# A new hand-over-hand order for the same operations of a recurrence-and-gated-MLP kernel

## The chip, the cores and the metric

The kernel runs on one core of a Trainium2 chip. The metric is the device time of one execution in microseconds (us). Below, TensorE is also PE, VectorE is DVE, ScalarE is ACT, GpSimd is POOL, and SyncE (SP) is the engine whose queue issues nearly all DMAs.

## The reference

Four batches, eight heads, 768 steps, head size 48. First a gated linear recurrence, then an MLP with a spatial mix:

```python
for t in range(S):
    state = alpha[:, :, t, :, None] * state + einsum('bhd,bhe->bhde', k[:, :, t], v[:, :, t])
    y[:, :, t] = einsum('bhd,bhde->bhe', q[:, :, t], state)
x = y.transpose(0, 2, 1, 3).reshape(B, S, H * D)      # 4 x 768 x 384
h = maximum(x @ w_in, 0)                              # 384 -> 1024
u, v = h[..., :512], h[..., 512:]
v_n = (v - mean(v)) / sqrt(var(v) + 1e-6)             # over the features
v_s = einsum('ts,bsd->btd', w_spatial, v_n) + b_spatial[None, :, None]
out = (u * v_s) @ w_out                               # 512 -> 384
```

## The kernel before

**Chunks and pairs.** The recurrence is done in chunks of 128 steps, six to a batch, 24 in all (number `i`). The first eight chunks are loaded and worked on two at a time as pairs 0 to 3 (`pair`, one 384 KB load for each of alpha, k, q, v), the other 16 singly (`first`, 192 KB loads). For a chunk the kernel loads alpha, k, q and v (`ac`, `kc`, `qc`, `vc`), takes the logarithm of alpha (`ln`), sums it along the steps with a matmul (`cum`), takes the exponent with both signs (`einv`, `eexp`), scales k and q (`kt`, `qt`), casts v (`vb`), transposes k and q on TensorE (`tr`, `trk`) and copies the transposes out of PSUM (`ev`), multiplies them (`sc`), masks the product (`m`), and makes `y` from the masked product (`ya` for a pair), v and the state before the chunk. The state goes on by `upd` (matmul), `z` (add), `S` (decay) and `sb` (cast). A `y` is cast (`xs`), transposed (`xt`) and copied (`xe`) as the MLP's input. Names of pair operations carry the pair and the half: `qtp/0/1`.

**The MLP.** For each batch: `v` (relu of the second half, token by feature), its statistics `bn`, `rs` and normalisation `vn`, `u` (relu of the first half, feature by token), `s` (the spatial matmul, with the bias added on the way out of PSUM), `g` (product with u), and `o` (the last matmul) with its store `st`. The very last output tile is split in two halves `oh`. Weights come in six 768 KB pieces: `w_in` in two halves, `w_sp` in three, `w_out`; each piece is cast to bf16 in slices (`cast`), and the spatial weights are transposed (`wt`, copied out by `we`).

**What sets the order.** Nothing is left to a scheduler. The kernel builds a list of 1141 operations, each with the engines that may do it, what it depends on, and a function that emits its instructions. Then `replay` walks through the string `PLAN`. A word such as `D65` means: emit operation 65 on the engine of the letter, P TensorE, D VectorE, A ScalarE, G GpSimd, S SyncE's issue of a DMA, Q its landing (emits nothing). So the order of the words of one letter is the order of that engine's instructions; how words of different letters are mixed changes nothing but the turn of shared buffers. Every engine works through its own list in order and waits where an operand is late.

**Buffers that tie the engines.** PSUM is eight banks taken in turn (`bank`), in the order of TensorE's list: a matmul whose bank still waits for its reader waits too. Loads go into three rotating buffers for each of alpha, k, q and v (a buffer holds two chunks), so a load can be issued only when the buffer's last reader is through. SyncE issues loads and stores in one list.

**Idle matmuls.** A word of TensorE may carry numbers, as in `P43:512:512:192`. Before that operation's matmuls, `bank` emits one fp32 matmul of `junk` by `junk` for each number, with so many columns; its result is overwritten. In the profile these matmuls are line L188.

```python
        for cols in fill:
            n = cols // 4
            nc.tensor.matmul(
                out=flat[:, 0:cols].rearrange("p (a b) -> p a b", a=4), lhsT=junk,
                rhs=junk[:, None, 0:n].to_broadcast([128, 4, n]), start=True, stop=True)
```

**Lines that are met below.** L435 issues the pair loads, L446 is `lnp`, L455 `cump`, L463 `einvp`, L484 `qtp`, L477 `ktp`, L547 `updq`, L577 `sc` of a pair, L588 its mask, L604 `ya`, L822 all matmuls of the MLP, L834 `wt`, L887 `bn`, L919 `vn`, L968 the exit of `s`, L981 `g`, L198 copies on ScalarE, L200 copies on VectorE and GpSimd.

Of the kernel before, what the change touches and what calls it, by code (L numbers as in the profile page):

```python
# [9 lines left out]
FP32 = mybir.dt.float32  # L10
# [44 lines left out]
LETTERS = {"P": "PE", "D": "DVE", "A": "ACT", "G": "POOL", "S": "SP", "Q": "DMA"}  # L55

PLAN = """
G32 S34 Q33 S36 G0 S38 S40 Q35 D1 Q37 S94 A42 D2 Q39 S96 P43:512:512:192 P53:64 A44 A45 G46 Q41 S98 A54 A55 D47 G56
D57 P51:512 Q95 P49 S100 P59:64 P61 A58 G48 D60 A50 D52 P63:192 Q97 S163 A62 P247 D65 A102 P71 D248 P74 D72 A64 Q99
S167 P103:96 G66 P113 D73 A104 A114 D68 D76 A115 Q101 P249 S165 G116 A105 A250 D117 G106 D107 P121:512 Q164 S169 D75  # L60
A122 P111:64 G67 P109 D112 P119 A110 G69 D120 Q168 S4 P131:192 D70 P134 G108 P77 G118 D133 G3 P123:128 A171 Q166
D132 S307 D125 A124 A78 P172 D136 P81 G126 P182 A173 Q170 S9 D135 P79 A183 D127 A82 P137 A174 Q5 D128 A184 S311 P142
D176 P138 G185 P83 A139 D175 A80 P140 A84 D186 P178 A143 P180 D179 A177 G187 P188 P190 Q308 S309 D189 G129 P144 P192
D181 A145 D191 A141 G6 D194 A193 A8 P197 D7 Q10 P200 G195 D199 P85 S14 A315 G196 D198 P157 A86 G130 D201 P316 A158
P146 D202 Q312 A317 D159 A318 P203 A147 P204 P208 D87 P88 A205 Q310 A209 G11 P206 D12 P326 A89 D13 P210 A207 D320
P151 S18 Q15 A211 D148 S313 P212 A327 S367 G319 A328 P324 D152 P223 A213 D330 G329 P215 A160 D90 A325 Q19 P334 S371
P322 A216 P221 D162 G16 A224 D217 P153 A222 P332 G17 A91 D323 P229 A335 P225 D92 Q314 S22 D231 A154 P149 D93 A333
G20 D214 P232 A226 P227 A150 Q368 D230 S369 P155 D234 A228 D161 A233 P235 D21 Q372 A218 S409 D237 P238 A236 D219
P344 G321 A156 Q23 D239 P255 S446 D220 G331 P259 D345 A375 P376 D346 P336 A377 A378 A380 P260 D338 Q370 S373 A240
D381 P256 A337 D261 A24 P263 G339 Q410 D257 S411 P264 D25 G379 P241 Q447 D341 P347 A242 S448 D265 P251 A243 G342  # L70
D349 Q374 P244 P383 G340 S413 A245 D246 P252 D348 A417 G262 P275 Q412 A385 S415 D253 P276 D384 G258 A382 Q449 P350
D277 A454 S450 P390 A351 G343 P267 D391 Q414 P418 S480 G278 D392 P354 P352 A419 P279 Q416 A353 S26 G421 P268 A355
P386 A420 A422 P356 D269 Q451 G266 P393 S482 A357 D387 P280 A394 D423 G388 P455 Q481 D281 S484 P395 A457 P425 A456
G389 P361 D427 A424 Q27 D397 G458 A396 S452 P358 D426 A459 A362 D460 P398 G254 A359 D363 P428 A399 P462 G270 P432
D429 A488 P271 D433 A463 G430 Q483 S577 P401 D464 P489 D434 A28 G31 P407 Q485 A490 G30 S486 D400 P272 A492 P435 A402
G491 Q453 D29 P405 S581 A436 D273 P283 G282 A408 D493 Q578 S579 P437 P469 A284 G274 D438 P495 A406 D470 P403 Q487
A496 S611 G461 D471 P287 A439 G431 A497 Q582 D404 P291 S583 A288 D360 P465 P498 Q580 A585 S648 P472 D466 A292 D500
P586 G494 A364 P440 Q612 G467 D499 A587 S690 P295 A473 G468 D366 A588 A590 Q584 S615 P474 A441 G589 P501 D475 D591
P299 Q649 A502 D442 S728 A476 P503 A296 P593 G592 P477 A619 Q691 D505 D504 S613 A300 D594 P517 D365 A478 Q616 P596
D595 S650 P506 A443 D597 A479 D518 P513 Q729 D445 S652 A507 P600 D444 P620 A508 D602 Q614 P519 S692 A621 P533 D509  # L80
A656 P303 Q651 S694 A514 D601 P515 A510 Q653 A622 P525 A698 D512 S617 D511 A624 P529 G623 D516 A520 Q693 P657 S654
P534 A304 D625 G598 A659 A658 P526 D535 Q695 G599 A661 S732 P699 D527 P530 A701 A700 G660 P545 Q618 A703 D531 S730
A736 P627 G536 P603 D629 Q655 P546 S762 A604 D704 G528 P537 A628 D662 Q733 P538 S696 D547 G626 P605 P664 D539 G702
A606 P634 Q731 A607 P630 S766 A665 P541 D631 G663 A666 D635 P737 Q763 G632 P542 S858 A738 D636 G548 A739 P671 A741
P706 Q697 D543 S892 P667 A708 G532 P608 D742 A707 D672 Q767 P521 S764 G740 A609 P637 D633 A770 P549 Q859 A638 S734
D668 P522 D673 P550 Q893 G705 D523 S862 P639 P744 D551 A640 P713 G524 A641 Q765 D746 P674 A745 S860 D714 P771 G669
A675 P642 D715 A772 Q735 G670 S768 A774 P751 P676 A643 P553 G540 D678 Q863 D677 A866 S864 D775 P709 P716 A554 G773
D752 P679 Q861 A717 S929 D753 A900 G544 P557 A680 D710 Q769 D610 S896 P777 G711 A558 P718 P867 A743 G712 Q865 P561
D719 A869 D779 S933 A868 D720 A681 P747 G552 D778 P686 Q930 D644 S894 P721 A871 G870 A562 P754 D748 Q897 A722 D872
S971 P565 G749 A755 D687 G750 A645 Q934 P780 P874 S931 A566 D782 P756 P569 G776 A757 A723 Q895 D781 G873 S975 P573  # L90
D876 A758 A875 P783 D724 Q972 S898 P682 A784 A570 P881 D646 Q932 P785 P759 S973 D787 A786 D883 A574 P788 A937 Q976
D882 S935 A760 P796 D683 A789 P684 Q899 D761 S1012 A797 P877 P800 A685 D790 Q974 A725 P901 S1008 P688 A903 A801 D647
P794 A979 Q936 D726 S1042 P938 A791 D727 P798 D878 A902 Q1013 D792 P810 A940 A905 S1046 D793 G904 P802 A939 D795
P980 Q1009 D906 G879 S1010 P803 A981 P811 G941 A799 D804 Q1043 A942 P806 S977 D689 A982 G805 A984 P807 D812 Q1047
P884 S571 D943 P822 G907 A885 D985 P823 G813 Q1011 D808 S1044 P908 P886 G983 P945 A910 D887 Q978 P814 D909 S1014
A888 D824 P911 A946 G809 P815 D912 Q572 A947 P889 S1048 D816 G944 A1016 Q1045 S575 D880 P987 A890 G817 P915 P952
A988 D916 Q1015 P1017 G913 P830 A1050 D989 A1019 G914 P834 A1018 D917 Q1049 A1021 P1051 D953 G825 P838 A1052 Q576
D954 A835 P948 G1020 P831 A1054 D949 P918 D832 G950 P818 A919 D1022 G986 P819 A839 D1055 G951 P920 P1024 D820 A921
P994 A1025 G1053 D922 P990 P826 D996 A1026 P955 G1023 D995 P827 G833 A956 D991 P1031 D828 P957 P1057 G992 A959 D1032
P923 A958 G821 A1059 D1033 P960 A924 G829 P997 A1058 D925 P967 A998 G993 P1027 A961 P999 P1060 D1028 A968 P842 D962  # L100
G1029 A1000 A1001 P963 G1030 A843 D1061 P1002 A1056 S844 D1062 A964 P1034 S305 A1003 D891 P850 S836 Q845 A1035 S840
P1063 D1004 Q306 P846 A1064 Q837 A926 P1065 P1036 A847 P965 D1067 Q841 D1037 A1038 D1066 P854 D928 D966 P1068 A851
D927 A1005 P969 A1069 D1006 P1074 D1007 P1039 D1070 P1078 A1040 P1080 A855 D1041 P1076 A970 S856 P1090 S297 D1075
A1071 P1094 S285 D1079 A1077 Q857 P1082 S289 D1072 P1106 Q298 D1073 S301 D1081 P1086 Q286 S567 P1087 Q290 S563 P1083
D1088 Q302 S852 P1095 G1089 Q568 P1091 S559 D1096 P1102 Q564 S293 D1092 G1097 P1098 D1084 Q853 S848 P1103 D1093 Q560
G1085 S555 P1099 D1104 Q294 P1107 D1105 P1113 Q849 D1100 Q556 P1117 A1114 D1108 G1101 P1110 D1109 S1115 A1118 P1111
S1119 P1121 D1112 Q1116 P1137 A1122 Q1120 P1125 D1138 S1123 P1133 S1139 A1126 P1129 D1134 Q1124 S1127 S1135 A1130
Q1140 S1131 Q1128 Q1136 Q1132
"""


# [13 lines left out]
def kernel(  # L125
# [14 lines left out]
    B, H, S, D = q.shape  # L140
# [20 lines left out]
    io_pool = ctx.enter_context(tc.tile_pool(name="io", bufs=IO))  # L161
# [146 lines left out]
    T = {}  # L308
# [319 lines left out]
    def first(i):  # L628
# [3 lines left out]
        st = T[i]  # L632
        P = float(10 * i)

        def load(name, src):
            def emit(_):
                if i % 2 == 0:
                    T[i + 1][name + "2"] = st[name + "2"] = io_pool.tile([128, 2, H, D], FP32, name=name)
                t = st[name] = st[name + "2"][:, i % 2]
                nc.sync.dma_start(out=t, in_=src[b, :, t0:t0 + C, :].rearrange("h s d -> s h d"))  # L640
            return emit
# [453 lines left out]
    for b in range(B):  # L1095
        for c in range(NCH):
            i = b * NCH + c
# [50 lines left out]
```

## Time and profile before

| what | value |
|---|---|
| median of 3 runs | 145.32 us (145.25 to 145.40) |
| span of the profiled execution, first to last instruction | 142.9 us |
| granted TensorE clock | 1.000 |
| busy: TensorE matmuls | 132.9 us, 93% |
| busy: VectorE | 122.2 us, 85% |
| busy: ScalarE | 108.2 us, 76% |
| busy: GpSimd | 86.0 us, 60% |
| DMA moved | 28.6 MB, mean 200 GB/s |

The profile does not give a separate time for the profiled execution. Its span is 142.9 us, and the runs lie 2.4 us above that; this is what start and end of a program add around the first and last instruction. The spans of matmuls overlap each other, as they are pipelined, so a busy share of TensorE in the nineties means that a next matmul nearly always follows at once.

### The profile page before, as it was taken

How to read it: one execution, taken by the hardware profiler on the slowest of the kernel's cores; microseconds unless marked ns; L12 is line 12 of the kernel's file. 1: busy time of each engine (PE TensorE's matmuls, PEld its weight loads, DVE VectorE, ACT ScalarE, POOL GpSimd, SP SyncE). 2: the span in 40 equal slices, each digit the busy share in tenths (PEclk: the TensorE clock that was granted, in tenths of full speed). 3: DMA queues.
4: the chain of work that ended last, by engine and by line, in shares of the span. 5: the costliest groups of instructions: out<-in, count | busy, mean ns of one | idle time of the engine just before them, and what ended most of it. 6: DMA issues, size and time to landing. Idle time of an engine off the chain costs nothing.

```text
span 142.9 us, 4962 instructions
## 1 busy us (share of the span) xinstructions
PE 132.9 (93%) x1910; PEld 83.7 (59%) x1923; DVE 122.2 (85%) x290; ACT 108.2 (76%) x280; POOL 86.0 (60%) x147
## 2 busy tenths in 40 slices
PE   7978977999799999999999999999999999999990
PEld 3464857456465666665655666656666666556460
DVE  6759998998989799989789999889889989776950
ACT  3567398899976799999987889999878688760131
POOL 6945853748317999971288879910999994003700
PEclk9999999999999999999999999999999999999999
DMA  4999989999998999999899999999999103229645
GB/s 115 268 261 265 250 201 327 334 322 328 251 224 163 213 276 161 203 176 198 145 205 192 164 209 162 208 143 206 187 156 222 55 7 137 86 98 338 229 150 180
DMA packets 89000, 28.64 MB, mean 200 GB/s; under 512 B 83728, under 2 KB 87440, under 8 KB 88976
## 3 DMA queue, kind: packets, MB, share of 16 engines
q1 hardware_dynamic: 88944, 28.32, 92.0%
q8 instruction: 15, 0.25, 0.8%
q14 instruction: 9, 0.07, 0.2%
q0 software_dynamic: 32, 0.00, 0.0%
HBM read 23.60 MB, written 4.72 MB: 198 GB/s over the span
## 4 chain that ended last, share of the span: by engine, by line
PE 70%; DMA 10%; SPq 6%; ACT 6%; DVE 3%; issue 2%; ACTq 0%
PE bank L822 50%; DMA ac<-in_alpha_dram 10%; SPq L435 6%; PE bank L748 3%; PE bank L713 3%; PE bank L776 2%; PE bank L660 2%; ACT v_sb L204 2%; PE bank L734 2%; PE bank L770 2%; PE bank L392 2%; DVE stats L887 1%; DVE vn L919 1%; ACT x_sb L198 1%; PE bank L663 1%
## 5 line engine op out<-in xcount | busy, mean ns | idle before, releaser
L822 PE MATMUL bank<-w_spT,vn 128*128 128x384 bf16 x192 | 36.3, 326 | 0.0
L981 POOL TENSOR_TENSOR gT<-vsb,uT 128x384 bf16<-128x384 f32 x28 | 25.8, 928 | 14.2 <-DVE vsb L968 13.5
L822 PEld LDWEIGHTS <-vn 128*128 128x128 bf16 x192 | 16.8, 97 | 10.5 <-DVE vn L919 0.2
L684 POOL TENSOR_TENSOR kt<-kc,binv 128x384 bf16<-128x384 f32 x16 | 14.8, 924 | 12.6 <-ACT bc L679 6.6
L759 DVE TENSOR_TENSOR ptm<-bank,mask 128x512 bf16<-128x512 f32 x32 | 20.8, 683 | 0.6 <-PE bank L748 0.6
L822 PE MATMUL bank<-xT,w_in 128*128 128x384 bf16 x96 | 19.7, 326 | 0.1
L968 DVE TENSOR_TENSOR vsb<-bank,bsp_bc 128x384 f32<-128x384 f32 x31 | 16.6, 552 | 3.0 <-PE bank L822 1.6
L822 PE MATMUL bank<-w_out_sb,gT 128*128 128x384 bf16 (+1 forms) x100 | 18.6, 319 | 0.0
L822 PE MATMUL bank<-w_in,xT 128*128 128x512 bf16 x59 | 16.9, 379 | 1.1 <-issue 0.3
L198 ACT COPY kqT<-bank 128x512 bf16<-128x512 bf16 x26 | 14.8, 592 | 1.3 <-PE bank L713 0.8
L338 POOL TENSOR_TENSOR state<-state,bc 128x192 f32<-128x192 f32 x20 | 10.4, 518 | 8.8 <-ACT bc L553 6.4
L887 DVE BATCH_NORM_STATS2 stats<-v_sb 128x6 f32<-128x512 bf16 x20 | 13.7, 683 | 1.4 <-ACT v_sb L204 1.4
L198 ACT CAST x_sb<-bank 128x384 bf16<-128x384 f32 x24 | 11.5, 485 | 2.2 <-PE bank L776 1.9
L204 ACT ACTIVATE v_sb<-bank 128x512 bf16<-128x512 f32 x20 | 11.6, 601 | 1.6 <-PE bank L822 1.5
L822 PEld LDWEIGHTS <-gT 128*128 128x128 bf16 x100 | 8.9, 97 | 5.6 <-POOL gT L981 0.4
L200 POOL CAST sbd<-state 64x192 bf16<-64x192 f32 x32 | 10.9, 341 | 1.7
L822 PEld LDWEIGHTS <-w_in 128*128 128x128 bf16 x96 | 8.3, 97 | 5.3 <-issue 0.4
L198 ACT COPY xT<-bank 128x192 bf16<-128x192 bf16 (+1 forms) x25 | 8.7, 384 | 2.9 <-PE bank L392 2.6
L919 DVE TENSOR_SCALAR vn<-v_sb,mvs,rstd 128x512 bf16<-128x512 bf16 x24 | 9.8, 437 | 0.7 <-ACT rstd L912 0.7
L588 DVE TENSOR_TENSOR ptm<-bank,mask 128x512 bf16<-128x512 f32 x16 | 10.3, 676 | 0.0
L188 PE MATMUL bank<-junk 128*128 128x512 f32 (+4 forms) x24 | 9.3, 490 | 1.1 <-DVE junk L234 1.1
L200 DVE COPY kqT<-bank 128x512 bf16<-128x512 bf16 x22 | 9.0, 417 | 1.5 <-PE bank L505 0.9
(131 smaller groups left out, 288.2 us busy)
## 6 DMA issues: line engine op xcount, KB each, us to landing
ac<-in_alpha_dram SPq DMA_DIRECT2D x16, 192.0 KB, 4.6
qc<-in_q_dram SPq DMA_DIRECT2D x16, 192.0 KB, 4.7
kc<-in_k_dram SPq DMA_DIRECT2D x16, 192.0 KB, 4.8
vc<-in_v_dram SPq DMA_DIRECT2D x16, 192.0 KB, 4.3
raw_w<-in_moe_w_spatial_dram SPq DMA_DIRECT2D x3, 768.0 KB, 6.8
out_dram<-raw_w SPq DMA_DIRECT2D x11, 192.0 KB, 2.1
out_dram<-o_sb SPq DMA_DIRECT2D x9, 192.0 KB, 2.0
ac<-in_alpha_dram SPq DMA_DIRECT2D x4, 384.0 KB, 6.6
```

What stands on the lines that cost most here:

```text
L198: nc.scalar.copy(out=out, in_=in_)
L200: ENG[eng].tensor_copy(out=out, in_=in_)
L204: nc.scalar.activation(out=out, in_=in_, func=AF.Relu)
L338: ENG[eng].tensor_tensor(out=st["state"], in0=st["state"], in1=st["bc"][:, :, None].to_broadcast([128, HP, D]), op=ALU.mult)
L588: nc.vector.tensor_tensor(out=st[f"ptm{par}"][:, s], in0=st[f"pt{s}{par}"], in1=mask2[:, par], op=ALU.mult)
L684: ENG[eng].tensor_mul(out=k_blocks(kt3)[:, :, :, 0:D], in0=quad(st["kc"]), in1=st["binv"])
L759: nc.vector.tensor_tensor(out=st["ptm"][:, s], in0=st[f"pt{s}"], in1=mask4, op=ALU.mult)
L822: return lambda ps: nc.tensor.matmul(out=out(ps), lhsT=lhsT(), rhs=rhs(), start=start, stop=stop)
L887: nc.vector.bn_stats(out=stats, in_=d["v_sb"][:, tt, :])
L919: nc.vector.tensor_scalar(out=d["vn"][:, t, :], in0=d["v_sb"][:, t, :], scalar1=d["mvs"][:, t, 0:1], scalar2=d["rstd"][:, t:t + 1], op0=AL ...
L968: nc.vector.tensor_tensor(out=hold["vs"], in0=ps[:, 0:TH], in1=bsp_bc[:, th, :], op=ALU.add)
L981: ENG[eng].tensor_tensor(out=bt[b]["gT"][:, dsl, cols], in0=hold["vs"], in1=bt[b]["uT"][:, dsl, cols], op=ALU.mult)
```

## The change

The string `PLAN` is replaced by another one for the same 1141 operations. 95 of them move to another engine, all between VectorE, ScalarE and GpSimd (34 from ScalarE to VectorE, 28 the other way, the rest to or from GpSimd). TensorE, SyncE and the number of loads and stores keep their operations; their order is new. The idle matmuls become 11 with 3,876 columns in all, in place of 12 with 3,040. In the function `load` of the single chunks, the pair's shared tile is now made by whichever of its two chunks is loaded first, where it was always the even one.

The first words of both plans, and the last ones:

```diff
-G32 S34 Q33 S36 G0 S38 S40 Q35 D1 Q37 S94 A42 D2 Q39 S96 P43:512:512:192 P53:64 A44 A45 G46 Q41 S98 A54 A55 D47 G56
-D57 P51:512 Q95 P49 S100 P59:64 P61 A58 G48 D60 A50 D52 P63:192 Q97 S163 A62 P247 D65 A102 P71 D248 P74 D72 A64 Q99
...
+S34 Q35 S94 Q95 G32 Q33 S36 Q37 G0 S38 Q39 D1 D2 A42 S98 Q99 P43:512:512:512:460 P53 A44 A102 A54 D56 S96 Q97 P103:492
+A45 A104 G46 S40 Q41 P113 S163 Q164 D47 P247 P49:196 P249 P51:296 P59 A55 A114 D57 S100 Q101 P61 A115 A105 A60 A62
...
         def load(name, src):
             def emit(_):
-                if i % 2 == 0:
-                    T[i + 1][name + "2"] = st[name + "2"] = io_pool.tile([128, 2, H, D], FP32, name=name)
+                if name + "2" not in st:
+                    T[i - i % 2][name + "2"] = T[i + 1 - i % 2][name + "2"] = io_pool.tile([128, 2, H, D], FP32, name=name)
                 t = st[name] = st[name + "2"][:, i % 2]
```

In names, the lists begin like this.

```
SyncE before  ac/0 kc/0 qc/0 vc/0 ac/2 kc/2 qc/2 vc/2 ac/4 qc/4 kc/4 vc/4 w_in/1 ac/6 w_in/0 qc/6 kc/6 w_sp/0 w_sp/1 vc/6 ...
SyncE after   ac/0 ac/2 kc/0 qc/0 qc/2 kc/2 vc/0 ac/4 vc/2 kc/4 qc/4 vc/4 w_in/1 ac/6 w_in/0 kc/6 qc/6 w_sp/0 vc/6 w_sp/1 ...
PE before     junk cump/0/0 junk cump/0/1 junk tr/q/0/0 tr/k/0/0 junk tr/k/0/1 tr/q/0/1 junk updq/0 bb/0 sc/0/0 sc/0/1 junk cump/1/0 cump/1/1 ...
PE after      junk cump/0/0 cump/0/1 junk cump/1/0 cump/1/1 bb/0 junk tr/k/0/0 bb/1 junk tr/q/0/0 tr/k/0/1 tr/q/0/1 tr/q/1/0 tr/q/1/1 sc/0/0 ...
```

Later in SyncE's list, a store of batch 0 stands before `kc/19` and `qc/19`, and four stores stand right before the last load `vc/23`, where before one store stood three places ahead of it. At the end, the two halves of the last tile leave PSUM on ScalarE where they left on VectorE, the last matmul is `oh/3/5/0` where it was `o/3/4`, and of batch 3's products `g`, VectorE does `g/3/1/0`, `g/3/2/0`, `g/3/2/1`, `g/3/0/1` and GpSimd the other three.

## The prediction, made blind

> **What bounds the kernel now.** I read the page first: who is busy, and in which slices.
>
> ```profile
> span 142.9 us, 4962 instructions
> PE 132.9 (93%) x1910; PEld 83.7 (59%) x1923; DVE 122.2 (85%) x290; ACT 108.2 (76%) x280; POOL 86.0 (60%) x147
> ...
> PE   7978977999799999999999999999999999999990
> DMA  4999989999998999999899999999999103229645
> ```
>
> TensorE is gapless from about 36 us (slice 11) to 139; before that it has holes. The DMA engines are full until 107 us. So there is an opening that waits for data, and a stretch of 100 us in which TensorE's work decides. The chain of waits, second, confirms it:
>
> ```profile
> 10.13 7.69 DMA ac<-in_alpha_dram
> 19.17 6.97 DMA ac<-in_alpha_dram
> ...
> 33.58 0.61 ACT v_sb L204
> 34.21 0.71 DVE stats L887
> ...
> 38.28 0.48 DVE w_row L200
> 38.80 0.35 PE bank L834 x12
> ...
> 123.63 15.93 PE bank L822 x97
> 139.58 0.48 ACT raw_w L198
> ```
>
> The end hangs on loads to 26 us, on ScalarE to 34, on VectorE to 38.8, then on TensorE, and one copy and one store. Third, windows of the time, TensorE and VectorE in the first two columns after the mean:
>
> ```profile
> core 0: us, PE busy (x) PEld busy (x) DVE busy (x) ACT busy (x) POOL busy (x), PEclk, DMA share, GB/s
> 20.00:25.00 5.00, 3.97 (x114) 3.52 (x117) 4.53 (x13) 4.33 (x12) 2.12 (x4) 1.00 0.92 276
> 35.00:40.00 5.00, 4.24 (x80) 2.37 (x73) 4.96 (x16) 4.83 (x14) 1.78 (x3) 1.00 1.16 271
> 50.00:60.00 10.00, 9.84 (x160) 6.55 (x158) 9.55 (x22) 9.28 (x24) 9.75 (x16) 1.00 1.08 218
> ...
> 17.00:20.40 3.40, 2.50 (x73) 2.01 (x69) 3.35 (x8) 2.30 (x6) 1.77 (x5) 1.00 0.94 228
> ```
>
> VectorE is 99% busy when it holds TensorE at 35 to 40 us, and all engines are over 92% at 50 to 60: a slip of any of them reaches TensorE. Fourth, the timeline of the first microseconds, for the idle matmuls:
>
> ```profile
> 1.05 4.04 PE L188 MATMUL bank<-junk 128*128 128x512 f32 x6 [1.05 <-DVE junk L234]
> 5.33 0.32 PE L455 MATMUL bank<-la,le_pair 128*128 128x384 bf16 x1 [0.23 <-ACT la L446]
> ...
> 6.14 1.02 PE L188 MATMUL bank<-junk 128*128 128x512 f32 x2
> ```
>
> Both 512-column calls are cold at the start (1.7 us each), but one at 6.14 takes 0.86.
>
> **A measure for the rest.** TensorE's operations, each at its pace in the full stretches (0.163 us per 384 columns, so 0.49 for `u`, 0.98 for `s`, 0.65 for `o` and `v`; 0.28 `trk`, 0.30 `sc`, 0.37 `y`), add up to 121.5 us in either order. The first `s` stretch shows the offset: `cum/8` starts at 40.26 with 24.5 us of that work done, so TensorE runs 15.8 us behind a start without waits. It ends at 139.55, 18.1 behind. Hence 15.8 are lost in the opening, 0.5 between work 24.5 and 34, 1.3 from there to 113, 0.5 in the tail. The change can only alter these four. The edit of `load` emits the same DMAs. Of the 95 operations that change engine, the sums by row durations are 114.2 us for VectorE (was 116.0), 103.4 for ScalarE (101.9) and 85.8 for GpSimd (86.1): small against their place in the lists.
>
> **The opening.** Idle matmuls: 1,996 columns stand before `cump/0/0` instead of 1,216. Two calls are cold (3.4 us), 972 columns then warm (1.6): 1.05 to 6.1, where before it was free at 5.1 and started at 5.33. Later idle calls total 1,880 columns, 3.1 us warm, and stand where TensorE waits for loads.
>
> Loads: the first twelve are of one size and wait for nothing, so the order only exchanges landings. From the issue times and semaphores those are 4.3, 5.9, 7.4, 8.9, 10.4, 11.9, 13.4, 14.9, 17.8, 19.2, 20.6, 22.6. Thus `ac/2` comes at 5.9 (was 10.4), `ac/4` at 14.9 (17.8), but `vc/0` at 13.4 (8.9) and `vc/2` at 17.8 (14.9); `vc/4` stays at 22.6, `w_in/1` at 24.7, `w_in/0` at 28.3. I walked the four lists through these, with row durations (start to start: ptm 0.60, qt 0.47, kqT copies 0.42 to 0.48, x_sb 0.38, v_sb 0.49, stats and mvs 0.82, vn 0.32; GpSimd kt 0.91, state 0.51) and 0.2 us from a matmul's end to its reader. New waits: ScalarE stands until 13.4 for `vc/0` and from 15.8 to 17.8 for `vc/2` (before, it stood just as long for `ac/4`). `updq/0` starts at 14.0 instead of 9.5, `updq/1` at 18.4 (17.2), `ya/0` at 19.2 (16.5), `ya/1` at 22.1 (19.9). Then `vc/4` equalises: `sc/2` 24.1 (24.3), the first `v` 25.5 (25.2), the last pair-2 mask done on VectorE at 27.8 (28.0). ScalarE has the four `v` relus done at 29.0 (30.5), but four other operations, 1.5 us, behind them instead of ahead. At 36 to 40 the walk finds `wt/2` waiting until 38.9 for its bank (VectorE copies `we/0/1` out after two masks), `we/2/0` at 40.0, and the first `s` at 40.15 with 24.5 done: offset 15.65. **Opening: 0.15 us better, give or take 0.7.** A lost load slot here costs 1.4.
>
> **Work 24.5 to 34.** For each TensorE operation I summed the work on another engine's list up to the last operand it needs, and subtracted TensorE's own work ahead. VectorE before: 7.8 at `wt/3`, 7.4 at the first `s`, 7.3 at `s/0/2/1`, 7.2 at `sc/8`. After: 6.9, 6.6, 6.5, 6.4, and 4.7 to 6.4 between. The largest is what TensorE must trail by. The walk leaves VectorE 8.3 us behind its list, so TensorE may be at 15.2, and is already at 15.65: these holds go. ScalarE needs 4.6 (was 4.0) at one place and 1.7 (2.4) from work 28 on. GpSimd needs 1.2 to 1.5 us more up to 48, having four casts more, but starts chunk 8 at 39.5 instead of 42.5. I take 0.1 lost where 0.46 was: **0.35 better.**
>
> **Work 34 to 113.** VectorE's lead falls further, 5.5 to 4.0 at 36, 5.9 to 3.7 at 40, 5.1 to 3.4 at 48, nothing by 80. The explicit holes of TensorE in the trace here are about ten of 0.10 to 0.16 us; five or six show no releaser, and I leave these, 0.8, as they are: the change's words say that instruction reads are spaced, but the same matmuls have to be read. Copy hops from TensorE and back (`y`, `xs`, `xt`) fell short of cover by 0.2 us in sum before and nowhere after. Loads: the least spare before need is 1.1 us (`qc/10`), as before; stores put ahead of `qc/20` and `vc/23` delay these by 1 and 3 us, with 3 and 5 to spare. A moved wait: `vc/23`'s issue now queues behind stores of `o/0/0` to `o/1/2`, done by 94. **0.3 better**; between 0.9 better (all but the reads gone) and 1.5 worse (one bad hold per batch of 0.4).
>
> **Tail.** Before, TensorE waits for GpSimd's gT at 134.12 (0.17) and small holes follow. After, the first three `o` find their g done 0.15 us early, and only `oh/3/5/1` waits 0.05 for VectorE. **0.3 better.** Then the last matmul is a half tile: its copy queues behind `o/3/4`'s on ScalarE, 0.4 us, and its store behind the other's issue, 0.5; with 1.8 to land, the same 2.4 us after the last matmul as now. Cost nothing.
>
> Sum: 0.15 + 0.35 + 0.3 + 0.3 = 1.1 better; I round to 1.0 for what such a walk forgets. Span 141.9. The runs lie 2.4 above the span of the profiled execution: 144.3.
>
> [...] Between 15.1 and 18.5 us the new order gives TensorE 1.25 us of work (in the window row 17.0 to 20.4 before, about the least busy, 2.50 of 3.40, and still warm: L604 takes 0.57 for 32 matmuls at 16.5 and at 20.2. The clock column says 1.00 in the cold first microseconds too and can't tell). [...]
>
> **The rivals.** *Main case*, 144.3, itself 143.6 to 144.9: chance 0.50. [...] 0.14. *New holds in the long stretch*: all engines run at 92% and ScalarE's lead at work 80 worsens by 1.2 us, GpSimd's by 1; with 1.5 lost and the tail and opening kept, 145.9. 0.20. *Nothing moves*: TensorE's 121.5 us are the same, and the holds gone come back as others, 145.3. 0.10. *More is gained*: the opening 0.7 better than walked, the holds gone: 143.2. 0.06.
>
> **How the numbers follow.** A difference of 0.2%, 0.3 us, is about what a measurement here can tell. Faster: 0.06 and all but 0.01 of the main case, 0.55. Same: 0.11. Slower: 0.34. The range from 143.4 to 146.3 leaves out the tips of both sides.
>
> **What would show it.** Right: `cump/0/0` at 6.1, the first `s` (L822 with vn) within 40.15 +- 0.7, TensorE's last matmul at about 138.5, no DVE releaser over 0.3 us before TensorE after 42, a gT wait of under 0.1 at the end. [...]

## The result and the profile after

The changed kernel takes 149.92 us (median of five runs, 149.80 to 151.84), beside 145.25 us for the kernel before on the same chip: ratio 1.035, 95% interval 1.030 to 1.040. The forecast was 144.3, with a range up to 146.3. So the change costs 4.7 us where 1.0 was to be gained, and the range did not hold it.

One thing must be known to read its time rightly. The exits of `s` turn through four buffers `vsb` in the order of the plan's words, and in the new plan seven of the 31 products `g` come after a fifth exit has taken their buffer again. These seven (`g/0/1/0`, `g/0/3/0`, `g/1/2/0`, `g/1/2/1`, `g/2/2/0`, `g/2/1/1`, `g/3/0/0`) are ordered behind another tile's exit and read its values, so the new order makes them wrong. It costs little time: in the trace only `g/3/0/0` waits for the other exit (0.35 us at 140.64), the other six start as soon as GpSimd is free. The order before has none of that.

The page of the changed kernel, totals and slices:

```profile
span 150.1 us, 4973 instructions
PE 139.8 (93%) x1921; PEld 85.4 (57%) x1921; DVE 122.7 (82%) x290; ACT 107.8 (72%) x278; POOL 85.4 (57%) x149
...
PE   7998988899969999999999999999999989999981
PEclk9999999699996999999999999999999999999999
DMA  3999999986999999999988999999998026450044
```

TensorE's busy time is up by 6.9 us, for the same matmuls apart from the idle ones, and in the clock row are two dips that before did not have. The profiled execution is the longest of the five (151.84, clock 0.977, both dips). The other four, with clocks of 0.984 to 0.988, took 149.8 to 150.1. By their clocks they had one dip each (half a clock for 3.41 us of 148 gives 0.988); which of the two, a clock alone does not say.

Windows of the same execution show the dips as PEclk of 0.73 and 0.72:

```profile
core 0: us, PE busy (x) PEld busy (x) DVE busy (x) ACT busy (x) POOL busy (x), PEclk, DMA share, GB/s
25.00:30.00 5.00, 3.80 (x55) 2.46 (x52) 3.18 (x6) 2.35 (x6) 1.38 (x4) 0.73 1.11 283
40.00:45.00 5.00, 3.82 (x119) 2.73 (x110) 4.93 (x14) 4.55 (x15) 0.51 (x1) 0.94 1.01 251
45.00:50.00 5.00, 5.00 (x30) 2.56 (x30) 3.38 (x8) 1.07 (x2) 4.11 (x7) 0.72 0.91 174
115.00:125.00 10.00, 9.02 (x156) 5.66 (x155) 9.61 (x21) 7.09 (x20) 8.42 (x14) 1.00 0.22 72
```

Before, the first and the third of these stretches read:

```profile
25.00:30.00 5.00, 4.48 (x79) 2.42 (x70) 4.93 (x11) 4.45 (x11) 2.99 (x7) 1.00 1.14 318
45.00:50.00 5.00, 5.00 (x101) 3.25 (x94) 4.10 (x8) 4.01 (x10) 4.62 (x9) 1.00 1.20 206
```

From 45 to 50 us TensorE is busy all the time, but at a clock of 0.72. The clock record itself has 0.5 from 27.31 to 30.73 and from 44.38 to 47.79, each 3.41 us long, so each costs 1.7 us of work: at the end of the first, matmuls of 512 columns (L821) start 0.43 us apart, right after it 0.22. What stands ahead of the two dips is in the timeline:

```profile
25.20 0.47 PE L576 MATMUL bank<-kqT 48*64 48x128 bf16 x19
26.87 0.41 PE L576 MATMUL bank<-kqT 48*64 48x128 bf16 x13 [1.20 <-issue]
...
42.92 0.35 DVE L199 COPY w_spT<-bank 128x384 bf16<-128x384 bf16 x1
43.33 0.33 PE L833 MATMUL bank<-ident,w_row 64*128 64x64 bf16 x11 [1.18 <-DVE w_spT L199]
44.22 1.31 PE L821 MATMUL bank<-w_spT,vn 128*128 128x384 bf16 x4
```

(Line numbers after are one lower than before.) The first hole lies in the middle of one operation, `sc/2/0`, after 19 of its 32 matmuls, and no operand releases it. It is a late read of instructions, as e3 below shows. Both kernels have 15 of these DMAs of 16 KB in the trace's queue "instruction". In before they start 250 of TensorE's matmuls and weight loads apart on average (239 of these had begun at the first read, 3,735 at the last). Some 700 have begun at the hole. As an estimate from these counts, each read brings some 256 instructions and is wanted some 256 ahead of them, the second thus at about 450. In the changed kernel the second read starts at 24.21, 0.12 us before `w_in/1` (768 KB, issued from 16.82) has landed at 24.33, and ends at 25.37; that load's packets are on the DMA engines from 19.9 on. By this estimate TensorE had passed the place from which the read is wanted at 19.85 (449 begun), and has used up what it had at 25.4 (702). It goes on at 26.87, 1.5 us after the read has ended; what fills this time the trace does not show (in e2 it is 1.3). Before, by the same estimate, the read was wanted at 17.7 (442); it started at 19.39, ahead of these packets (20.06 there), and was done at 20.35, and its instructions were needed at 24.7 (700). The second hole is the wait of `wt/2` for its bank that the walk had found (VectorE copies `we/0/1` after two masks).

The third and fourth places of loss lie late, on VectorE:

```profile
116.17 1.79 POOL L980 TENSOR_TENSOR gT<-vsb,uT 128x384 bf16<-128x384 f32 x2
117.18 1.78 DVE L199 CAST sbd<-state 64x192 bf16<-64x192 f32 x2
117.92 0.93 POOL L683 TENSOR_TENSOR kt<-kc,binv 128x384 bf16<-128x384 f32 x1
119.40 0.81 PE L821 MATMUL bank<-w_out_sb,gT 128*128 128x384 bf16 x4 [0.32 <-DVE state L332]
120.66 0.33 PE L769 MATMUL bank<-sbd,kqT 128*128 128x96 bf16 x4 [0.45 <-DVE vsb L967]
...
140.64 2.10 POOL L980 TENSOR_TENSOR gT<-vsb,uT 128x384 bf16<-128x384 f32 x2 [0.35 <-DVE vsb L967]
140.94 2.22 DVE L980 TENSOR_TENSOR gT<-vsb,uT 128x384 bf16<-128x384 f32 x2
144.35 0.89 PE L821 MATMUL bank<-w_out_sb,gT 128*128 128x192 bf16 x5 [0.52 <-DVE gT L980]
```

The two casts of `sb/19` take 1.78 us, and the two products at 140.94 take 2.22, both while GpSimd does work of its own (`g` and `kt` in the rows above). In before's trace the same cast takes 0.25 to 0.87 on VectorE, and a product 0.55 to 0.91 (minimum, median and maximum in ns):

```profile
L200 DVE CAST sbd<-state x8: 253/359/873, 16.2 to 107.1; 64x192 bf16<-64x192 f32 x8
L981 DVE TENSOR_TENSOR gT<-vsb,uT x3: 548/558/907, 132.7 to 135.5; 128x384 bf16<-128x384 f32 x3
```

The slow casts each ended 0.11 to 0.12 us behind an operation of GpSimd: at 118.07 and 118.96, where GpSimd's ended at 117.96 and 118.84; before's slowest at 107.95, GpSimd's at 107.83. Before's cast at 106.81, which started 0.05 us ahead of that operation of GpSimd, took 0.26.

In the prediction's measure (TensorE's offset, that is time minus work done) it reads so; e1 and e3 are the first and third experiment below:

| at work done | before | after | e1 | e3 |
|---|---|---|---|---|
| 24.5 us | 15.9 | 19.7 | 15.5 | 15.8 |
| 34 | 16.3 | 21.1 | 15.9 | 15.6 |
| 96 | 17.7 | 22.4 | 17.7 | 17.5 |
| 99 | 17.7 | 24.1 | 19.0 | 19.1 |
| 113 | 17.6 | 23.9 | 18.8 | 19.0 |
| 119 | 18.1 | 25.1 | 20.1 | 20.2 |

(The profiled execution of after has both half-clock windows; a run with one of them should have some 1.7 less from there on.)

### The profile page after: what moved, and what is told of

It is laid out like the page before. It is cut to its first block, busy times and chain, and to the rows that moved or that the text cites. A ratio compares the mean times of both kernels' runs of the same rounds, so it can differ in the third digit from the quotient of the medians.

```text
span 150.1 us, 4973 instructions
## 1 busy us (share of the span) xinstructions
PE 139.8 (93%) x1921; PEld 85.4 (57%) x1921; DVE 122.7 (82%) x290; ACT 107.8 (72%) x278; POOL 85.4 (57%) x149
## 4 chain that ended last, share of the span: by engine, by line
PE 59%; DVE 19%; ACT 7%; issue 5%; SPq 4%; DMA 2%; POOL 1%; ACTq 0%; DVEq 0%; POOLq 0%
PE bank L821 36%; PE bank L187 6%; DVE stats L886 3%; DVE vn L918 3%; SPq L1036 2%; SPq L639 2%; PE bank L747 2%; DVE uT L205 2%; DVE ptm L587 2%; PE bank L712 2%; PE bank L775 2%; DMA vc<-in_v_dram 2%; PE bank L769 2%; DVE ptm L758 2%; PE bank L733 1%
## 5 line engine op out<-in xcount | busy, mean ns | idle before, releaser
L821 PE MATMUL bank<-w_spT,vn 128*128 128x384 bf16 x192 | 38.0, 337 | 0.1
L980 POOL TENSOR_TENSOR gT<-vsb,uT 128x384 bf16<-128x384 f32 x27 | 24.5, 926 | 16.8 <-DVE vsb L967 16.6
L821 PEld LDWEIGHTS <-vn 128*128 128x128 bf16 x192 | 17.4, 100 | 11.4 <-issue 1.7
L967 DVE TENSOR_TENSOR vsb<-bank,bsp_bc 128x384 f32<-128x384 f32 x31 | 16.3, 550 | 5.4 <-PE bank L821 5.4
L821 PE MATMUL bank<-xT,w_in 128*128 128x384 bf16 x96 | 19.7, 325 | 0.2 <-ACT kqT L197 0.2
L821 PE MATMUL bank<-w_in,xT 128*128 128x512 bf16 x72 | 19.8, 398 | 0.0
L821 PE MATMUL bank<-w_out_sb,gT 128*128 128x384 bf16 (+1 forms) x100 | 18.7, 320 | 0.9 <-DVE gT L980 0.5
L197 ACT COPY kqT<-bank 128x512 bf16<-128x512 bf16 x28 | 15.8, 604 | 0.9 <-PE bank L504 0.9
L199 POOL CAST sbd<-state 64x192 bf16<-64x192 f32 x38 | 13.1, 346 | 2.0
L821 PEld LDWEIGHTS <-gT 128*128 128x128 bf16 x100 | 8.8, 97 | 7.2 <-DVE gT L980 1.1
L187 PE MATMUL bank<-junk 128*128 128x512 f32 (+7 forms) x22 | 11.7, 651 | 1.1 <-DVE junk L233 1.1
L197 ACT COPY xT<-bank 128x192 bf16<-128x192 bf16 (+1 forms) x18 | 7.0, 400 | 6.9 <-PE bank L391 3.6
L821 PEld LDWEIGHTS <-w_in 128*128 128x128 bf16 x96 | 8.4, 97 | 5.5 <-DVE xT L199 0.3
L918 DVE TENSOR_SCALAR vn<-v_sb,mvs,rstd 128x512 bf16<-128x512 bf16 x24 | 10.9, 475 | 0.3 <-ACT rstd L911 0.2
L821 PEld LDWEIGHTS <-xT 128*128 128x128 bf16 x72 | 6.5, 102 | 6.6 <-issue 1.6
```

The costliest lines, as they stand in the source:

```text
L187: nc.tensor.matmul(out=flat[:, 0:cols].rearrange("p (a b) -> p a b", a=4), lhsT=junk, rhs=junk[:, None, 0:n].to_broadcast([128, 4, n]), st ...
L197: nc.scalar.copy(out=out, in_=in_)
L199: ENG[eng].tensor_copy(out=out, in_=in_)
L821: return lambda ps: nc.tensor.matmul(out=out(ps), lhsT=lhsT(), rhs=rhs(), start=start, stop=stop)
L918: nc.vector.tensor_scalar(out=d["vn"][:, t, :], in0=d["v_sb"][:, t, :], scalar1=d["mvs"][:, t, 0:1], scalar2=d["rstd"][:, t:t + 1], op0=AL ...
L967: nc.vector.tensor_tensor(out=hold["vs"], in0=ps[:, 0:TH], in1=bsp_bc[:, th, :], op=ALU.add)
```

## The experiments

The edits are in the words of the plan; names stand for the numbers. The kernels ran in four groups on different chips, each beside the kernel before: e1 to e4 (before 145.26), e5 to e8 (before 145.97), e9 to e12 (before 145.27), e13 (before 145.29). Between groups the ratios compare, not the times. Executions of one kernel come with a dip (mean clock about 0.988) and without one (1.00), so a median can mix the two: two of e2's four runs had a clock of 1.00 and took 146.6, the other two had 0.988 and took 148.0 and 148.1. Every kernel but e2, e9, e10, e12 and e13 reads seven `vsb` buffers late, as the changed kernel does.

**e1_before_opening: the old opening, the new rest.**

```diff
-lists of after from the first word on
+lists of before up to wt/3, then all that is left in the order of after
```

> The order before up to its operation wt/3 (TensorE at about 38 us), the new order for all that is left. Theory A (the opening of the new order is the loss: an instruction read of TensorE late behind the load w_in/1, and half-clock windows after holes): first s matmul at 39 to 40.5 us, clock 1.000, no hole over 0.5 us before 40, 145.0 or less; if the new long stretch is as good as I summed, 144.3. Theory B (the new long stretch itself is slower): first s as early, but 147 to 149 us, the loss spread over 45 to 125 us.

147.30 us, ratio 1.014 (1.011 to 1.017), clock 1.00. The first `s` is at 40.17, with the offset of before (15.5 beside 15.9). The rest alone loses 2.0 us, nearly all of it at the two late places: holes of 0.32 at 114.66 and 0.45 at 115.92, and 0.52 at 139.25.

**e2_after_opening: the new opening, the old rest.**

```diff
-lists of after from the first word on
+lists of after up to the first s, then all that is left in the order of before
```

> The new order up to its first s matmul, the order before for all that is left. Theory A: the first s matmul at 42 to 44.5 us, one or two half-clock windows (clock 0.976 to 0.988), 148.5 to 150.5 us. Theory B: 145 to 146.5 us, since the opening's delay is then made up for.

147.32 us, ratio 1.015 (1.009 to 1.021). At the seam the masks `m/3/1` and the sum `z/7` read banks that a later matmul has taken; the instructions are the same. The read starts at 24.09 and its hole is 2.01 us, the hole before `wt/2` 1.18. The late holes are gone. The profiled execution has no dip although its hole at the read is the longest of all. So the loss has two parts, one in the rest (2.0 us, e1) and one in the opening: 1.4 us in the runs without a dip, 2.8 in those with one, as all runs of the changed kernel have. As e2 drops some waits at its seam, its time is good for this rough split only.

**e3_read_shift: the read moved away from the loads.**

```diff
-P(cump/0/0):512:512:512:460
+P(cump/0/0):(64 matmuls of 1 x 1):512:460
```

> The new order; of the four idle matmuls before cump/0/0 two are replaced by 64 matmuls of one column and one row, so that TensorE's list has 120 more instructions there in about the same time. Theory A1 (the hole of 1.2 us at 25.7 is a late read of the next 256 instructions, wanted when instruction 450 is passed and queued behind w_in/1): the read is wanted 120 instructions earlier, at 17 to 18 us instead of 19.9, and starts by 21 instead of 24.2; the hole in the middle of sc/2/0 goes or, if one is left, it stands 120 instructions earlier in TensorE's list (near tr/q/2/0 or ya/1); no half clock at 27 to 31; 1 to 2.5 us less than the new order, 147.5 to 149. Theory A2 (the hole is a wait for an operand or a bank in sc/2/0 that the trace does not name): the hole stays in sc/2/0, 149.5 to 150.

147.17 us, ratio 1.017 (1.011 to 1.023). 120 instructions more bring the second read to 19.01, ahead of `w_in/1`'s packets. In the timeline of this kernel `sc/2/0` and `sc/2/1` run through:

```profile
23.91 0.57 PE L553 MATMUL bank<-vbp,kt 64*128 64x48 bf16 x16
24.41 0.64 PE L583 MATMUL bank<-kqT 48*64 48x128 bf16 x32
24.99 0.51 PE L374 MATMUL bank<-ident,x_sb 128*128 128x128 bf16 x6
25.33 0.56 PE L194 MATMUL bank<-junk 128*128 128x200 f32 x2
25.73 2.54 PE L828 MATMUL bank<-w_in,xT 128*128 128x512 bf16 x10
```

The first `v` is at 25.73 (the walk said 25.5), the first `s` at 40.45 (40.15), and there is no dip (one of the other three runs has a clock of 0.988). The hole before `wt/2` is still 1.19, with no dip behind it. So the late read and one dip are worth 149.92 - 147.17 = 2.75 us, about what a hole of 1.2 and one window of 1.7 make.

**e4_copy_first: VectorE's copy `we/0/1` ahead of the masks `m/3/0`.**

```diff
-D(m/3/0/0) D(m/3/0/1) D(we/0/1)
+D(we/0/1) D(m/3/0/0) D(m/3/0/1)
```

> The new order with one move: VectorE copies we/0/1 out of its bank before the two masks m/3/0/0 and m/3/0/1, not after them. Theory A: wt/2 gets its bank 1.2 us earlier, the hole at 42.1 to 43.3 is under 0.3 us, and no half-clock window follows at 44 to 48: 1.0 to 2.5 us less than the new order, 147.4 to 149. Rival (the masks are then as late and hold TensorE in their place, or the hole does not matter to the clock): 149.5 to 150, with a half-clock window still at 44 to 48.

No verdict on the time: four runs from 147.75 (clock 1.000) to 151.59 (clock 0.977). The profile answers for the place: the hole is 0.28 instead of 1.18, but `sc/3/1` now waits 0.26 and 0.35 for the masks, and no dip follows in this execution (two others, with clocks of 0.976 and 0.977, must have had two dips). The read's hole (1.54 here) and the dip behind it stay. Of the 0.9 us gained, 0.6 are gone within a microsecond.

**e5_sb_pool: the casts `sb/19` from VectorE to GpSimd** (from e3).

```diff
-D(qt/23) D(sb/19) D(z/21)         G(g/2/0/1) G(kt/23)
+D(qt/23) D(z/21)                  G(g/2/0/1) G(sb/19) G(kt/23)
```

> Starts from e3_read_shift (147.17 us, TensorE's last matmul at 141.75) and moves one operation: the two state casts sb/19 go from VectorE's list (between qt/23 and z/21) to GpSimd's, between g/2/0/1 and kt/23. Theory P (VectorE and GpSimd exclude each other in some pairs of operations): on VectorE these two casts took 1.77 us, where the same form took 0.25 each elsewhere, and each ended as an operation of GpSimd ended. On GpSimd they take 0.35 each; VectorE's z/21 starts 1.8 us earlier, TensorE's holes of 0.31 at 114.5 (released by state) and 0.45 at 115.7 (released by vsb) go, the last matmul ends at 140.5 and the time is 146.0. Rival L (the order of the lists is what is late, not the pairing): GpSimd's kt/23, sb/20 and state slip by the 0.7 us that they take, a hole released by POOL takes their place, and the time is 147.2 or more.

146.88 us beside 145.97, ratio 1.005 (1.001 to 1.009), where e3 had 1.017. On GpSimd all 40 casts take the same time:

```profile
L206 POOL CAST sbd<-state x40: 337/343/345, 19.1 to 122.4; 64x192 bf16<-64x192 f32 x40
```

Between work 96 and 99 the loss is 0.2 us (e3 1.65). At this place it went as theory P said, and the slow casts above ended as operations of GpSimd did; why they are slow there is not shown. A part of L holds too: GpSimd is later by those casts, and a new hole of 0.72 before `y/23`, released by its `sb/22`, gives 0.7 back.

**e6_tail_apart: the tail's products out of each other's way** (from e3).

```diff
-G(g/3/3/0) G(g/3/0/0)     D(g/3/2/1) D(s/3/0/1)
+G(g/3/0/0) G(g/3/3/0)     D(s/3/0/1) D(g/3/2/1)
```

> Starts from e3_read_shift (147.17 us) and moves two operations of batch 3's tail: g/3/0/0 goes ahead of g/3/3/0 on GpSimd, and s/3/0/1 (which reads PSUM) ahead of g/3/2/1 on VectorE, so that fewer products of the two engines coincide. Theory P: VectorE's g/3/2/0 and g/3/2/1, 1.03 and 1.26 us in the new order, take 0.55 to 0.75; TensorE's hole of 0.52 before the second half tile shrinks below 0.1, the last matmul ends at 141.1, the time is 146.5. Rival L (the chain from the last s over s/3/0/1 and g/3/0/1 is simply long): the hole stays at 0.5, 147.2.

A miss: 148.61, ratio 1.016 (1.012 to 1.020), as e3. The tail lost 1.5 us instead of 1.2. GpSimd's `g/3/0/0` did not start after its own exit `s/3/0/0`, done at 132.47, but at 136.96, right after `s/3/2/1` (136.81), whose tile is in its buffer by then. This led to the seven products named above.

**e7_all_four: e3, e4, e5 and e6 together.**

> The new order with all four repairs: instruction read shifted (e3), we/0/1 copied before the masks (e4), sb/19 on GpSimd (e5), the tail's products apart (e6). If the losses are separate: 147.17, less 1.2 for sb/19, 0.65 for the tail and 0.6 for the copy (its hole of 1.19 goes, some 0.6 comes back before sc/3/1) gives 144.7; first s at 39.9, last matmul at 139.3, no stretch of half clock. If the repairs overlap, that is, if another engine is next in line at each place, 145.5 or more.

147.16 us, ratio 1.009 (1.006 to 1.012), where 144.7, a ratio of 0.996, was expected. The first `s` is at 40.71, `y/23` waits 0.72 as in e5, the tail loses 1.5 as in e6. It is no faster than e5 alone (1.005, with an interval that overlaps): the moves of e4 and e6 repaired nothing here.

**e8_fill: one idle matmul more in the window before the dip** (from the changed kernel).

```diff
-P(updq/2)
+P(updq/2):512
```

> The new order as it is (149.92 us) with one idle matmul of 512 columns ahead of updq/2, at 24.4 us, in the 3.4 us before the half clock. It costs 0.86 us that lie beside the wait for the instruction read, which ends at 26.9 in any case. Theory G (the clock halves when too little of the array was used in a window of 3.4 us): with it that window is used to 0.48 instead of 0.23, the clock stays at 1.0 from 27 to 31 us, the first s is at 42.5 instead of 44.2 and the time is 148.2, if the second half-clock window (44.4 to 47.8) comes again, 147.0 or less if not. Rival H (the hole of 1.2 us itself does it): the hole stays, and so does the half clock after it; 149.9.

148.15 us, ratio 1.014 (1.010 to 1.019). Three of four runs have a clock of 0.997 or above, where none of the changed kernel's five had. That 148.2 was given is luck: theory G gave it for a second dip, which these three runs do not have, and 147.0 or less without one; the ratio puts the time at 147.3 beside a before of 145.25. Nor does the profile separate the two theories as cleanly as was meant. The read came at 23.58, and with the idle matmul in front `sc/2` started later, so that only 0.10 us of the hole was left:

```profile
23.82 1.09 PE L188 MATMUL bank<-junk 128*128 128x512 f32 x2
24.75 0.34 PE L539 MATMUL bank<-halves_of,la 128*128 128x2 bf16 x8
25.02 0.57 PE L547 MATMUL bank<-vbp,kt 64*128 64x48 bf16 x16
25.52 0.98 PE L577 MATMUL bank<-kqT 48*64 48x128 bf16 x32
```

Against H alone speaks e2, with the longest hole and no dip.

**e9_open_new_rest_old: the mended opening up to `updq/3`, then the old rest.**

> The new order with the instruction read shifted (e3) and we/0/1 first (e4) up to updq/3 (about 40.5 us), every list in the order of before from there on. It tells whether the new opening is worth anything once its two faults are gone. Theory A (the opening is better by what the walk said, and the loss sits in the read, the gate and the new rest): first s about 0.4 us before that of the kernel before, none of the holes at 114 to 118 and 139, ratio to before 0.997. Theory B (nothing is gained in the opening: one hole has only taken the place of another): ratio 1.000 or above, first s not earlier.

147.73 us, ratio 1.015 (1.012 to 1.019). Inconclusive: at this seam `wt/2` stands behind the cast of `w_sp/1`, which the old list has later on VectorE, a hole of 2.61 us at 40.89, and a dip follows it at 42.3. The cut made a loss of its own.

**e10_tail_early: buffers that are given back, and `g/3/0/0` at once** (from e3).

```diff
-hold["vs"] = vs_bufs[turn[1] % 4]; turn[1] += 1
+hold["vs"] = vs_bufs.pop(0)              # in the exit of s
+vs_bufs.append(hold["vs"])               # after its product g
-D(s/3/0/0) ... G(g/3/3/0) G(g/3/0/0)     D(g/3/2/1) D(s/3/0/1)
+D(s/3/0/0) G(g/3/0/0) ... G(g/3/3/0)     D(s/3/0/1) D(g/3/2/1)
```

> e3_read_shift with the tail of e6 mended: an exit of s takes a vsb buffer from a list to which its product g gives it back, in place of turning through four, and g/3/0/0 follows s/3/0/0 at once, ahead of g/3/3/0 on GpSimd; s/3/0/1 ahead of g/3/2/1 on VectorE as in e6. In e6 GpSimd's g/3/0/0 waited for s/3/2/1, four exits later, as this had taken the same buffer of the four. Theory P (what the tail lost is VectorE's products queueing behind GpSimd's): g/3/0/0 at 132.6, g/3/2/0 on VectorE takes 0.56 and g/3/2/1 below 1.0, the hole of 0.52 before the last tiles is below 0.2, TensorE loses 0.6 instead of 1.2 in the tail; ratio to before 1.012 where e3 had 1.0167. Rival L: the hole stays at 0.4 to 0.5, since s/3/0/1 and g/3/0/1 come too late in any case; 1.016. In the rest of the run nothing changes: the buffers given back by list make no new waits.

The time was off, the place right: 148.91, ratio 1.017 (1.013 to 1.020), but the tail from work 113 to 119 loses 0.35 us where e3 lost 1.22 (before 0.50), and the hole is gone. What was wrong is the sentence "In the rest of the run nothing changes": with a true give-back VectorE's `s/0/3/1` must wait for GpSimd's late `g/0/1/0`.

**e12_all_sound: all of it, and `g/2/2/1` behind `sb/22`**.

> All repairs of the new order: e7's (read shifted, we/0/1 first, sb/19 on GpSimd), e10's tail and buffers, and GpSimd's g/2/2/1 moved behind sb/22, which in e5 and e7 came late for y/23 (hole of 0.72). If each is a loss of its own: e7's ratio of 1.0089, less 0.004 for y/23 (0.2 of the 0.72 come back at o/2/4) and 0.005 for the tail, 1.000. If the new rest has no slack left anywhere, holes of the same size come up elsewhere and it is 1.007 or more.

146.37 us, ratio 1.008 (1.005 to 1.011). Both late places are cured: 0.2 us lost from 96 to 99 and none to 113, 0.35 in the tail. VectorE's four products `g` take 0.55 us each, in this answer for one tile (minimum, median, maximum in ns):

```profile
L986 DVE TENSOR_TENSOR gT<-vsb,uT x4: 548/550/558, 133.2 to 137.8; 128x384 bf16<-128x384 f32 x4
```

The largest wait that is left is seen in the timeline:

```profile
52.59 1.78 POOL L986 TENSOR_TENSOR gT<-vsb,uT 128x384 bf16<-128x384 f32 x2
53.53 0.56 DVE L973 TENSOR_TENSOR vsb<-bank,bsp_bc 128x384 f32<-128x384 f32 x1 [2.71 <-POOL gT L986]
54.01 0.41 DVE L206 COPY xT<-bank 128x192 bf16<-128x192 bf16 x2
54.48 0.37 PE L740 MATMUL bank<-vb,kt 128*128 128x48 bf16 x8 [1.74 <-DVE xT L206]
```

VectorE waits 2.71 us for the product, the copy of `xT` waits behind it in VectorE's list, and TensorE stands 1.74 us for that copy.

**e13_product_first: `g/0/1/0` ahead of `kt/9` on GpSimd** (from e12).

```diff
-G(S/8) G(kt/9) G(sb/8) G(vb/9) G(kt/10) G(g/0/1/0)
+G(S/8) G(g/0/1/0) G(kt/9) G(sb/8) G(vb/9) G(kt/10)
```

> e12_all_sound with one product moved: GpSimd's g/0/1/0 goes ahead of kt/9, where GpSimd stood idle for 0.6 us. In e10 and e12 VectorE's exit s/0/3/1 waited 2.7 us for this product to give its vsb buffer back, and TensorE 1.7 us at upd/9 behind it. Theory A (that wait is the price of buffers that are given back, and the only one): VectorE's wait falls below 0.3 us, TensorE's hole at 54.5 goes, and the time falls by 1.6 to 144.7 where e12 had 146.37; ratio to before 0.997, the last matmul at 139.2. Theory B (the next product is as late): VectorE waits for g/0/0/1 or g/0/3/1 instead, the hole moves on, ratio 1.005 or more.

144.87 us (twelve runs) beside 145.29 (seventeen), ratio 0.997 (0.994 to 1.0005), as theory A said. VectorE no longer waits for any product. The profiled execution is one of four with a dip and took 146.57; the eight runs with a clock of 0.995 or above took 144.08 to 144.97. It has the lowest ratio of all, but as its interval reaches 1, a gain over before is not shown.

## Why the prediction was wrong

**The step that failed first: "five or six show no releaser, and I leave these, 0.8, as they are ... the same matmuls have to be read".** The sentence stands under work 34 to 113; the walk through the opening has no instruction read in it, so a late one was put at nothing. The reads are the same in number, 15. What differed is when the second is wanted and what is on the DMA engines then. In the new order TensorE comes to the place where the second block is wanted at 19.85 (before 17.7, both by the estimate above), `w_in/1`'s packets run from 19.9, and the read started at 24.21, 0.12 us before that load had landed. Price: 1.2 us for the hole. e3 took it away with 120 more instructions at the head of TensorE's list, all else in the same order. The step needed the read's place among the loads.

**The clock.** The chance of 0.14 and the range's end at 146.3 were for a slower TensorE at 15 to 18 us. No run shows such a term: from 15.0 to 18.5 us after's trace has TensorE busy for 3.42 of 3.50 us at a clock of 1.00. The clock halved from 27.31 and from 44.38 us instead, at 1.7 us each, which the sum had at nothing. The longest gaps in the two windows of 3.41 us ahead of these dips are 1.20 and 1.18 us.

The traces show more. The clock record begins after the slow first matmuls (at 6.83 us in after, at 4.58 in before). From there on it changes only after whole multiples of 3.41 us, and the halvings inside a kernel each last 3.41 us. Six of them stand in the traces: two in after, one each in e4, e6, e9 and e13. Neither gap nor busy share tells them. TensorE was busy in 0.42 to 0.76 of the window ahead; e13's has no gap over 0.36 us, while a window of e10 with a gap of 1.74 and 0.49 busy did no harm. What does set them apart here is an estimate of how much of the array was in use: count each matmul's columns at the 0.163 us per 384 of the full stretches (fp32 at 0.86 per 512), times the share of the 128 rows and 128 columns that its record gives. The windows ahead of the six dips come to 0.23, 0.24, 0.27, 0.32, 0.38 and 0.38. All 14 traces have 566 windows at full clock: the 20 that half clock follows (14 of them at the end, where the work runs out) are at 0.38 or less, the other 546 at 0.38 or more. (The values move by up to 0.02 with the moment at which a matmul's time is taken to begin.) The window ahead of after's first dip (0.24) thus lies well below all those that no dip follows, that ahead of the second (0.38) on the edge.

**The opening and work 24.5 to 34** were right apart from these two and the start: the slow first matmuls (1.7 us per 512 columns, 0.86 later) lasted until 6.83 in after's profile (before 4.58), so `cump/0/0` came at 7.36 for the 6.1 predicted. Little of this is left behind the late read, as e2, whose `cump/0/0` came at 6.25, goes on at 26.50 and after at 26.87. With the read moved (e3) the first `s` is at 40.45 for a predicted 40.15 and the offset at work 34 is 0.7 below before's; the two steps had promised 0.5 together. The wait of `wt/2`, which the walk had end at 38.9, ends at 39.56 there and is 1.19 long.

**Work 34 to 113: predicted 0.3 better, measured 1.6 worse in the lists alone** (e1 goes from 15.9 to 18.8, before from 16.3 to 17.6: 2.9 lost for 1.3; of it 1.3 between work 96 and 99, 1.65 in e3). The mis-sized term is one cast. It was taken from the row's mean of 0.43 us; the two casts of `sb/19` took 0.88 each. That row's spread, 0.25 to 0.87 in before's trace, showed that the mean was of two different cases. e5 shows the price: 0.2 lost there instead of 1.65. It also shows that GpSimd's list has no 0.7 us to give at that place, which is why half came back at `y/23`. That engine times moved little in sum said nothing: what mattered was which operations of VectorE and GpSimd coincide. The rows show it: beside GpSimd's `g` and `kt` the cast took 0.88 us on VectorE, where it took 0.25 at the least, and beside `g` a product took 1.03 and 1.26, where it took 0.55. Why they are longer there is not shown. It was not looked for.

**The tail: predicted 0.3 better, measured 0.7 worse.** "The first three `o` find their g done 0.15 us early" was so: the hole is at the fourth. A product took VectorE 0.55 to 0.91 us before; `g/3/2/0` and `g/3/2/1` took 1.03 and 1.26, stacked with GpSimd's. GpSimd's `g/3/0/0` started at 140.64, 4.4 us after its own exit: most of it is its place behind `g/3/3/0`, the last 0.35 the buffer taken again. With both mended (e12) the tail is 0.15 better than before's, half of what was promised.

**The last tile** was neutral, as predicted. The rival of new holds in the long stretch (0.20, 145.9) was right in kind and near in size for the rest alone; it was not combined with a half clock, and the late read was no rival at all; the range ended at 146.3. The true time is the sum of two losses: 145.3 + 2.75 + 2.0 = 150. The 2.4 us between before's span and its runs are not what start and end of a program add: in the record each run is 1.73 to 1.85 us longer than its own span (145.31 for 143.5), and before's profiled execution was among the short ones. The forecast stays the same, as 145.3 less 1.0 is 144.3. Two readings of before's page were a slice early, without a bearing on the sum: it shows TensorE gapless from 39 us, not 36, and the DMA engines full until 111, not 107.

Settled are three places and their prices: the read with one dip 2.75 us, `sb/19` 1.3 to 1.65 (half to be had), the tail 0.7 to 0.85. With all of them mended, e13 is level with before, so no large loss is left unexplained. Of the gain of 1.0 some 0.4 may be there (144.87 beside 145.29), which is not clear of zero. Dips come without a late read too, in one of e3's four runs, four of e5's twelve and four of e6's six. The place of the windows may have a part in that: e12 and e13 run the same lists up to 49 us; the window near 37 us is cut 0.26 us later against the operations in e13, has 0.32 in use for e12's 0.40, and only e13 has the dip. Open is whether use of the array is the cause: no run changed it alone, as e8 shortened the hole too.

## What to carry to other kernels

When an order is changed, the spread of a row (minimum and maximum of one operation) says more than its mean: look at what the partner engine does while the long ones run. Here a cast on VectorE took 0.88 us beside GpSimd's work and 0.25 at the least, and moved to GpSimd 0.34 (e5). A wide hole that no operand releases, in the middle of one operation, is to be looked up among the instruction reads, and what is on the DMA engines when they are wanted: in e3, 120 instructions more brought one of them from 24.21 to 19.01, ahead of a load, and a hole of 1.2 us was gone. Before an order is trusted, follow each rotating buffer through the plan's text: a buffer that is turned by position is overtaken without a sign in most traces; here one wait, in e6, gave it away. And look at the clock row where TensorE does small matmuls: e13's clock halved for 3.41 us after a window in which TensorE was busy for 0.76 of the time.

## What was not expected of the hardware

- An instruction read of 16 KB that started late: in after wanted at 19.85 (estimate), started at 24.21, 0.12 us before the load `w_in/1` landed, with a hole of 1.20 us in TensorE's work; in before it started at 19.39, 1.7 us after it was wanted, with no hole.
- Six halvings of the clock, each for 3.41 us and at a price of 1.7 us, each after a window of 3.41 us in which TensorE was busy for 0.42 to 0.76 of the time but used the array to 0.38 or less (estimate). The mean clock of a run is near 1.000, 0.988 and 0.977 for none, one and two.
- The clock record begins, and the slow first matmuls end, at other times in other traces: at 4.58 us in before, 6.83 in after, 8.8 in e7. The windows of 3.41 us are counted from there.
- One instruction on VectorE, a cast of 64 x 192, took 0.25 us at the least and 0.87 at the most in before, 0.88 in after beside GpSimd's `g` and `kt`.
